# Filter planes of every second frequency group added on the Pool engine and turned in one pass a step later

## Chip, cores and metric

The kernel runs on one core of one Trainium2 chip. The metric is device time in microseconds (us): 248.57 us, the median of three runs (247.84 to 250.53). The core has five engines with queues of their own: TensorE (PE in the profile, with its weight loads as PEld), VectorE (DVE), ScalarE (ACT), GpSimd (POOL) and SyncE (SP), which here issues most DMA transfers. Each engine works through its instructions in the order in which the program wrote them; they wait for each other through semaphores.

## The reference

One transformer block on x of 2048 rows by 640 columns, in bf16:

```python
mod = (_silu(c) @ w_mod)                 # six vectors of 640: sa, ca, ga, sb, cb, gb
h = _layernorm(x, axis=-1) * (1 + ca) + sa
X = rfft2(h, axes=(rows, columns)) * (w_r + 1j * w_i)     # 2048 x 321 filter
x = x + ga * irfft2(X)
h = _layernorm(x, axis=-1) * (1 + cb) + sb
x = x + gb * ((_silu(h @ w_gate) * (h @ w_up)) @ w_down)  # 640 -> 1728 -> 640
```

So there is a spectral filter (a two-dimensional Fourier transform, a product with a complex filter, the transform back) and then a gated feed-forward layer.

## The kernel before

The transforms are matmuls with tables. Up to about 33 us the kernel normalises x and transforms its rows and most of the columns; from about 61 us to 79 us it transforms back and adds into x; after that come the gate, up and down products of the feed-forward layer. What is changed lies between, from 33 to 61 us, and is called the join here: for each column frequency l (0 to 80) the last small transform along the rows is made, the filter applied, and the first small transform back is made.

The frequencies lie in NG = 21 groups of mostly four (group 4 has two, group 5 three). The loop over g (line 764) writes the instructions out step by step; step g works on several groups at once:

- `mix(g+2)` (L581): one matmul of 192 columns per frequency, four per group, into two PSUM banks; the pair of banks is chosen by the group's parity.
- `prod(g+2, .., hl)` (L605, twice): DVE multiplies that result with the filter in `Wt` (tile rW) and writes three planes to SBUF, `PPs` (tile rM). With three real planes a complex product needs three multiplications instead of four; two sums of neighbouring planes are its real and its imaginary part.
- `stage_b(g)` (L613): PE turns the group's products, frequency on frequency, into bank 0 or 1 by a matmul with the identity. It makes two passes that accumulate, so that the planes are summed on the way: 8 matmuls of 128 columns. ACT copies the result to `Y2` (L616).
- `stage_c(u)` (L643) takes a unit of two groups two steps after its second group: 8 matmuls, into banks 6 and 7 for most units, which one copy (`evac`, L652, mostly ACT) then empties into tile rE.

Other work is laid between these:

- `turn` (L381, its copies L387 on ACT) mirrors raw filter rows, through banks 6 and 7. The last two, for l from 64 on, stand in step 6.
- `wsum` (L424, POOL) makes the third plane of the filter, a sum. `sp_gather` (L661, POOL) needs the result of a DMA transpose. L785 and L791 on POOL prepare tables of the next stage.
- `ga_mod` (L713, copy L719) in steps 1 and 2 uses banks 7 and 6.
- `mod_col` (L594): columns of sb and cb (five of each, five matmuls per column), all within `mix` of groups 18 to 20; those of gb in step 20.
- `sp_mm` / `sp_ev`: one special row frequency, in steps 5, 9, 11 and 13 (its parts 3, 0, 1, 2). Part 2 ends with a DMA from SP (L707); behind it in SP's order stand the loads of w_down, w_gate and w_up.
- `sp_w` / `sp_wc`: eight small transposes in step 3 with their copies (L445).

PP has four buffers, Y2 four, and the two banks of `stage_b` alternate. `presum` and `Qs` are in the code already, but `PRE` is empty, so nothing calls them.

Of the kernel before, what the change touches and what calls it, by code (L numbers as in the profile page):

```python
# [11 lines left out]
BF16 = mybir.dt.bfloat16  # L12
# [9 lines left out]
NC5 = 5  # L22
# [144 lines left out]
def adaln_block_kernel(ctx, tc, A_x, A_w_r, A_w_i, B_x, B_w_gate, B_w_up, B_w_down, c, w_mod, out):  # L167
    nc = tc.nc
# [19 lines left out]
    rE = _Region(big, "rE", 40960, "E")  # L188
# [37 lines left out]
    wm_r = rM.cut(12800, [NC5, 4, D])  # L226
# [16 lines left out]
    Wsp = rE.cut(34064, [3, 2, NT, 2], parts=81)  # L243
# [89 lines left out]
    if True:  # L333
# [87 lines left out]
        def wsum(lo, hi, rk, eng):  # L421
            for off in (lo, 161 - hi):
                v = [_rev(Wt, WP * i + 321 * rk + off, [[321, 8], [160, 2], [1, hi - lo]]) for i in range(3)]
                eng.tensor_tensor(v[1], v[2], v[0], ALU.add)  # L424
# [7 lines left out]
                                  sa4[:].unsqueeze(2).unsqueeze(3).to_broadcast([P, 4, 2, 8]))  # L432

        def sp_w():
            tp = psum[0:81, 4, 192:256].bitcast(BF16).rearrange("p (v h a k) -> p v h a k", v=2, h=2, a=2)
            for v in range(2):
                for hl in range(2):
                    for a in range(2):
                        o = 160 * (1 - a if hl else a)
                        nc.tensor.transpose(tp[:, v, hl, a], (Wrev if hl else Wrow)[:, v, o:o + 81], identb[0:16, 0:16])  # L440
            return tp

        def sp_wc(tp):
            for v in range(2):
                nc.vector.tensor_copy(Wsp[:, 2 * v].rearrange("p h k a -> p h a k"), tp[:, v])  # L445
            nc.gpsimd.tensor_tensor(Wsp[:, 1], Wsp[:, 0], Wsp[:, 2], ALU.add)

        cps = psum[:, 3, 0:NC5]
# [32 lines left out]
        dve, act = nc.vector.tensor_copy, nc.scalar.copy  # L481
# [51 lines left out]
    NG = len(groups)  # L533
    if True:
# [40 lines left out]
        def mix(g):  # L575
            ls = groups[g]
            n = len(ls)
            xps = banks(2 + 2 * (g % 2), 2, [4, 256])
            for i, l in enumerate(ls):
                B2, j = B2of[l][0:2]  # L580
                nc.tensor.matmul(xps[:, i, 0:192], lhsT=B2[:, j, :], rhs=KS2, start=True, stop=True)  # L581
                if i == 0:
                    for c5 in {NG - 3: (0, 1), NG - 2: range(NC5), NG - 1: (2, 3, 4)}.get(g, ()):
                        mod_col(psum[:, 2 + 2 * (g % 2), 192 + c5:193 + c5], wm_r[:, :, 1 + g % 2], c5)
            return xps

        def stage_a(g):
            xps = mix(g)
            prod(g, xps, 0)
            prod(g, xps, 1)  # L590

        def mod_col(o, w, c5):
            for k in range(NC5):
                nc.tensor.matmul(o, lhsT=w[:, k, 128 * c5:128 * c5 + 128], rhs=sc_col[:, k:k + 1],  # L594
                                 start=(k == 0), stop=(k == NC5 - 1))
# [11 lines left out]
        def stage_b(g, PP):  # L607
            n = len(groups[g])
            yps = banks((g + 1) % 2, 1, [4, 128])
            Q = Qs.pop(g, None)  # L610
            for ps in (1, 0) if Q is None else (0,):
                for i in range(n):
                    nc.tensor.matmul(yps[:, i, :], lhsT=_rev(PP if Q is None else Q, 64 * n * ps + i, [[n, 128]]), rhs=identb[:],  # L613
                                     start=(i == 0 and (ps == 1 or Q is not None)), stop=(ps == 0 and i == n - 1))
            Y2 = rY.cut(4096 if g == 4 else 1024 * (g % 4), [4, 128])
            nc.scalar.copy(Y2[:, 0:n, :], yps[:, 0:n, :])  # L616
# [28 lines left out]
        def evac(u):  # L645
            g, l0 = units[u][0], groups[units[u][0]][0]
            if g == NG - 2:
                nc.vector.tensor_copy(ep_views(l0, 4), banks(0, 1, [4, 128])[0:127].rearrange("p i q -> p q i"))
            elif g == NG - 1:
                nc.scalar.copy(ep_views(l0, 4), banks(1, 1, [4, 128])[0:127].rearrange("p i q -> p q i"))  # L650
            else:
                (nc.vector.tensor_copy if g == NG - 6 else nc.scalar.copy)(  # L652
                    ep_views(l0 // 4 * 4, 8), banks(4 if g == NG - 4 else 6, 2, [8, 128])[0:127].rearrange("p i q -> p q i"))

        B2sp = rE.cut(20480, [82])
# [7 lines left out]
        def gap(parts, i, w, b):  # L663
            return psum[0:parts, b + i // 2, 192 + 256 * (i % 2):192 + 256 * (i % 2) + w]
# [26 lines left out]
        def sp_ev(i, g):  # L691
            b = 2 + 2 * (g % 2)
            if i == 3:
                for h in range(2):
                    nc.vector.tensor_scalar_mul(SA[:, 41 * h:81 - 40 * (1 - h)], gap(128, h, 41 - h, b), 256.0)
            elif i == 0:
                for v in range(3):
                    nc.vector.tensor_tensor(PPsp[:, 64 * v:64 * v + 64], gap(81, v, 64, b),
                                            Wsp[:, v].rearrange("p h k a -> p (h k a)"), ALU.mult)
            elif i == 1:  # L700
                for h in range(2):
                    ls = slice(41 * h, 41 + 40 * h)
                    nc.scalar.copy(Y2sp[:, ls], gap(128, h, ls.stop - ls.start, b))
            elif i == 2:
                for h in range(2):
                    nc.scalar.copy(Osp[:, 40 * h:40 * h + 40], gap(128, h, 40, b))
# [57 lines left out]
        for g in range(NG + 1):  # L764
            if g == 9:
                nc.gpsimd.tensor_copy(sgnc[:], Kstab[:, 576:577])
# [12 lines left out]
            if 1 < g < NG - 2 and g + 2 in PRE:  # L779
                presum(g + 2)  # L780
            if g in (4, 9):
                wsum(64, 80, 8 * (g // 9), nc.gpsimd)
            if g in (11, 12):
                h4 = slice(4 * (g - 11), 4 * (g - 11) + 4)
                nc.gpsimd.tensor_scalar(sgn_H[:, h4, 1], sgn_H[:, h4, 0], sgnc[:, 0:1], 1.0, ALU.mult, ALU.mult)  # L785
            if g == NG - 3:
                nc.vector.tensor_copy(modcols[:, 2, :], psum[:, 2, 192:197])
                nc.vector.tensor_scalar_add(one_p_cb[:], psum[:, 4, 192:197], 1.0)
            if g in (14, 16):
                i = (16 - g) // 2  # L790
                nc.gpsimd.tensor_tensor(RI[:, i], RI[:, i], ga_bc[:], ALU.mult)  # L791
# [612 lines left out]
```

## Time and profile before

| | |
|---|---|
| median of the runs | 248.57 us (247.84 to 250.53) |
| the profiled execution: its time | 248.34 us |
| the profiled execution: its span | 246.3 us (2.0 us lie around it) |
| granted TensorE clock | 1.0 |
| busy in the whole span | PE 239.1, DVE 203.4, ACT 171.2, POOL 70.9 us |
| from 33 to 60 us | in most stretches of 1 us PE is busy for the whole of it; the weakest is 44 to 45 us with 0.69 |

A row of the timeline gives the start of a group of equal instructions, the time from its first start to its last end, the engine, the line and operation, output and input, how many, and in brackets how long the engine had stood idle before and what released it. PE's matmuls overlap each other: what a group costs PE is read from the start of one group to the start of the next. In lists by line, the three numbers are the shortest, middle and longest duration in ns.

### The profile page before, as it was taken

Reading aid. Unit: us, or ns where it says so; the run is one execution under the profiler, and the core shown is the slowest. Engines: PE = TensorE matmul, PEld = TensorE weight load, DVE = VectorE, ACT = ScalarE, POOL = GpSimd, SP = SyncE. Lnnn points to the kernel's source line nnn. Section 1 sums busy time; section 2 is a strip of 40 time slices with the busy share of each in tenths; the row PEclk is TensorE's granted clock in tenths of the full one; section 3 lists DMA queues with packets and bytes.
Section 4 is the critical chain, followed back from the end, with each engine's and each line's share of the span. In section 5 each row is a group of like instructions: output and inputs, shape, how many; then the busy total and the mean of one; then the engine's idle time right before and its main releaser. Section 6 shows DMA issues by size and latency. Waiting matters only on the chain.

```text
span 246.3 us, 6008 instructions
## 1 busy us (share of the span) xinstructions
PE 239.1 (97%) x2262; PEld 187.8 (76%) x2262; DVE 203.4 (83%) x479; ACT 171.2 (69%) x343; POOL 70.9 (29%) x116
## 2 busy tenths in 40 slices
PE   8889999999999999999999999999999999999994
PEld 2678889999998887788887778887765666656773
DVE  4798777897499996989989968788998777789964
ACT  4789887998988797588864588765247777773220
POOL 4368896660424523002004400001422000004400
PEclk9999999999999999999999999999999999999999
DMA  6999979969999999500005110202411000000111
GB/s 204 381 339 290 342 179 179 253 234 293 289 374 266 194 266 190 123 3 1 3 0 106 59 53 3 53 0 43 86 38 53 0 1 3 0 0 4 53 53 53
DMA packets 44142, 31.19 MB, mean 127 GB/s; under 512 B 21873, under 2 KB 41810, under 8 KB 44114
## 3 DMA queue, kind: packets, MB, share of 16 engines
q1 hardware_dynamic: 42176, 26.15, 39.8%
q0 software_dynamic: 1376, 4.26, 7.5%
q10 hardware_dynamic: 562, 0.41, 0.6%
q8 instruction: 17, 0.28, 0.5%
q14 instruction: 11, 0.09, 0.1%
HBM read 23.49 MB, written 2.62 MB: 106 GB/s over the span
## 4 chain that ended last, share of the span: by engine, by line
PE 84%; DMA 5%; DVE 4%; POOL 2%; ACT 2%; issue 1%; ACTq 0%; DVEq 0%; POOLq 0%
PE psum L1125 36%; PE psum L996 19%; PE psum L1095 6%; PE psum L613 4%; PE psum L973 3%; DMA rW<-rL 3%; PE psum L581 3%; PE psum L404 2%; DMA rX<-in_A_x_dram 2%; PE psum L643 2%; PE psum L1083 2%; DVE bn6a L337 2%; PE psum L729 1%; ACT rE L407 1%; DVE rE L369 1%; POOL rW L879 1%
## 5 line engine op out<-in xcount | busy, mean ns | idle before, releaser
L1125 PEld LDWEIGHTS <-rW 128*128 128x128 bf16 (+1 forms) x429 | 41.9, 98 | 12.6
L1125 PE MATMUL psum<-rW 128*128 128x256 bf16 (+1 forms) x247 | 42.2, 287 | 0.0
L1022 POOL TENSOR_TENSOR rM<-rM,rL 128x320 f32<-128x320 f32 x6 | 5.5, 909 | 97.1 <-ACT rL L1021 97.1
L996 PEld LDWEIGHTS <-rE 128*128 128x128 f16 (+1 forms) x196 | 18.9, 97 | 8.0 <-DVE rE L950 0.3
L605 DVE TENSOR_TENSOR rM<-psum,rW 128x384 bf16<-128x384 f32 (+2 forms) x42 | 20.5, 543 | 4.0 <-PE psum L581 2.7
L996 PE MATMUL psum<-rE 128*128 128x320 f16 (+1 forms) x147 | 22.9, 299 | 0.0
L1163 ACT COPY rX<-psum 128x384 f32<-128x384 f32 (+2 forms) x27 | 14.0, 519 | 7.4 <-PE psum L1125 7.3
L1156 ACT COPY rH<-psum 128x384 f32<-128x384 f32 (+2 forms) x27 | 14.0, 517 | 7.2 <-PE psum L1125 6.5
L1125 PEld LDWEIGHTS <-rE 128*128 128x128 f16 x156 | 15.3, 98 | 4.7
L1160 DVE TENSOR_TENSOR rH<-psum,rM 128x512 bf16<-128x512 f32 (+1 forms) x24 | 15.0, 624 | 4.1 <-PE psum L1125 2.2
L1179 ACT ACTIVATE rL<-psum 128x384 bf16<-128x384 f32 (+2 forms) x27 | 14.4, 533 | 5.4 <-PE psum L1125 3.4
L1164 DVE TENSOR_TENSOR rX<-psum,rX 128x384 f32<-128x384 f32 (+2 forms) x27 | 16.3, 604 | 1.6 <-ACT rX L1163 1.4
L1150 ACT COPY rM<-psum 128x384 f32<-128x384 f32 (+2 forms) x27 | 13.9, 516 | 4.0 <-PE psum L1125 3.9
L1271 DVE SCALAR_TENSOR_TENSOR rM<-psum,rX 128x640 f32<-128x640 f32 x16 | 13.1, 821 | 3.9 <-ACT rL L733 2.4
L1125 PE MATMUL psum<-rW,rE 128*128 128x256 bf16 (+1 forms) x78 | 15.6, 290 | 0.0
L1125 PE MATMUL psum<-rE,rY 128*128 128x256 f16 (+1 forms) x78 | 15.6, 290 | 0.0
L1180 ACT ACTIVATE rL<-rX 128x384 bf16<-128x384 f32 (+2 forms) x27 | 15.1, 558 | 0.0
L337 DVE BATCH_NORM_STATS2 bn6a<-rX 128x6 f32<-128x320 bf16 x30 | 13.1, 480 | 2.4 <-DMA rX<-in_A_x_dram 2.4
L1095 PE MATMUL psum<-rW 128*128 128x256 bf16 x130 | 14.4, 273 | 0.0
L965 DVE TENSOR_TENSOR rA<-psum,rM 128x320 bf16<-128x320 f32 (+1 forms) x27 | 12.1, 472 | 2.4 <-PE psum L973 2.3
L424 POOL TENSOR_TENSOR rW<-rW 128x256 bf16<-128x256 bf16 x20 | 13.5, 704 | 1.4 <-DMA rW<-in_A_w_r_dram 0.7
L1095 PEld LDWEIGHTS <-rW 128*128 128x128 bf16 x130 | 12.7, 98 | 1.5
(231 smaller groups left out, 633.0 us busy)
## 6 DMA issues: line engine op xcount, KB each, us to landing
rM<-in_w_mod_dram SPq DMA_DIRECT2D x4, 800.0 KB, 8.1
out_dram<-rA SPq DMA_DIRECT2D x31, 80.0 KB, 1.6
rX<-in_A_x_dram SPq DMA_DIRECT2D x6, 320.0 KB, 6.3
rA<-in_B_w_down_dram SPq DMA_DIRECT2D x2, 960.0 KB, 6.3
rY<-in_B_w_gate_dram POOLq DMA_DIRECT2D x2, 832.0 KB, 7.8
rW<-in_B_w_gate_dram SPq DMA_DIRECT2D x1, 1440.0 KB, 10.0
rW<-in_A_w_i_dram SPq DMA_DIRECT2D x2, 642.0 KB, 11.1
rW<-in_A_w_r_dram SPq DMA_DIRECT2D x2, 642.0 KB, 10.5
```

The lines of the kernel that those rows point to most:

```text
L337: nc.vector.bn_stats(bn6a[:, i % 2, k, :], x_sb[:, i, 320 * k:320 * k + 320])
L605: nc.vector.tensor_tensor(PPs[g][:, v0:v1, hl], xv[:, v0:v1, hl], in1, ALU.mult)
L996: nc.tensor.matmul(o, lhsT=lhs[rows(k), k], rhs=rhs[rows(k), k], start=start and k == ks[0], stop=stop and k == ks[-1], skip_group_check=True)
L1095: nc.tensor.matmul(gu[u], lhsT=Wgu[:, u, c5, ff * 128:(ff + 1) * 128], rhs=h2T[:, :, c5, :], start=(c5 == 0), stop=(c5 == NC5 - 1))
L1125: nc.tensor.matmul(o[:, f], lhsT=w, rhs=b, start=(start and f == 0 and i == 0), stop=(stop and f == len(groups[g]) - 1 and i == len(ops) - ...
L1150: nc.scalar.copy(c0, X)
L1156: nc.scalar.copy(c2, X)
L1160: nc.vector.tensor_tensor(c11, Z, c0, ALU.add)
L1163: nc.scalar.copy(c3, X)
L1164: nc.vector.tensor_tensor(c22, Y, c3, ALU.add)
L1179: nc.scalar.activation(g21, X, ACT.Silu, scale=-1.0)
L1180: nc.scalar.activation(g22, c22, ACT.Silu, scale=-1.0)
```

## The change

Three things are done to the join.

1. For the odd groups 3 to 17 (`PRE`), `presum` adds the two sums of planes on POOL into `Q` (tile rE, three buffers in turn), one instruction of 128x512 each, behind the group's products. `stage_b` of these groups then takes one pass, 4 matmuls instead of 8.
2. For groups 3 to 17, odd and even (`LAGS`), `stage_b` stands one step later: in step g it is written for group g-1. Step 3 has none and step 18 has two. `stage_c` stays where it was, so it comes one step behind the `stage_b` of its second group instead of two.
3. Other work moves. The last two `turn` go from step 6 to steps 7 and 9; `wsum` of rows 32 to 47 from ahead of the loop to step 2, that of 64 to 79 from steps 4 and 9 to 10 and 12; L785 from steps 11 and 12 to 14 and 18; L791 from 14 and 16 to 16 and 17; the ten `mod_col` of sb and cb from `mix` of groups 18 to 20 to those of groups 8, 10, 12, 14, 16 (one each), 18 (two) and 20 (three), now all in bank 3; `ga_mod` stands ahead of `stage_b`; `sp_w` goes from step 3 to step 5 with its transposes in bank 1, and its copies from DVE to ACT; the copies of the special row's parts 1 and 2 go from ACT to DVE, ahead of the step's products.

```diff
-            tp = psum[0:81, 4, 192:256].bitcast(BF16)...
+            tp = psum[0:81, 1, 256:320].bitcast(BF16)...
...
-                nc.vector.tensor_copy(Wsp[:, 2 * v]..., tp[:, v])
+                nc.scalar.copy(Wsp[:, 2 * v]..., tp[:, v])
...
-                    for c5 in {NG - 3: (0, 1), NG - 2: range(NC5), NG - 1: (2, 3, 4)}.get(g, ()):
-                        mod_col(psum[:, 2 + 2 * (g % 2), 192 + c5:193 + c5], wm_r[:, :, 1 + g % 2], c5)
+                    for c5 in {8: (0,), 10: (1,), 12: (2,), 14: (3,), 16: (4,), 18: (5, 6), 20: (7, 8, 9)}.get(g, ()):
+                        mod_col(psum[:, 3 + 2 * (g % 2), 448 + c5:449 + c5], wm_r[:, :, 1 + c5 // NC5], c5 % NC5)
...
-            Qs[g] = rE.cut(21504 + 1024 * (g % 3), [m])
+            Qs[g] = rE.cut(21504 + 1024 * (PRE.index(g) % 3), [m])
...
-                    nc.scalar.copy(Y2sp[:, ls], ...)
+                    nc.vector.tensor_copy(Y2sp[:, ls], ...)
...
-                    nc.scalar.copy(Osp[:, 40 * h:40 * h + 40], ...)
+                    nc.vector.tensor_copy(Osp[:, 40 * h:40 * h + 40], ...)
...
-        PRE = set()
-        SPG = (9, 11, 13, 5)
+        PRE = (3, 5, 7, 9, 11, 13, 15, 17)
+        LAGS = range(3, 18)
+        SPG = (9,11,13,5)
...
-        wsum(32, 48, 8, nc.gpsimd)
...
-                if g == 3:
-                    tp = sp_w()
-                stage_a(g + 2)
-                if g == 3:
-                    sp_wc(tp)
-                if g in SPG:
+                xps = mix(g + 2)
+                if g in SPG and SPG.index(g) in (1, 2):
                     sp_ev(SPG.index(g), g)
-            if 1 < g < NG - 2 and g + 2 in PRE:
+                prod(g + 2, xps, 0)
+                prod(g + 2, xps, 1)
+                if g == 2:
+                    wsum(32, 48, 8, nc.gpsimd)
+                if g in SPG and SPG.index(g) not in (1, 2):
+                    sp_ev(SPG.index(g), g)
+            if g + 2 in PRE:
                 presum(g + 2)
-            if g in (4, 9):
-                wsum(64, 80, 8 * (g // 9), nc.gpsimd)
-            if g in (11, 12):
+            if g in (10, 12):
+                wsum(64, 80, 8 * (10, 12).index(g), nc.gpsimd)
+            if g in (14, 18):
...
-            if g in (14, 16):
-                i = (16 - g) // 2
+            if g in (16, 17):
+                i = 1 - (16, 17).index(g)
                 nc.gpsimd.tensor_tensor(RI[:, i], RI[:, i], ga_bc[:], ALU.mult)
-            if g < NG:
-                Y2s[g] = stage_b(g, PPs.pop(g))
+            if 0 < g < 3:
+                ga_mod(320 * (2 - g), 8 - g)
+            for b in (g - 1, g):
+                if 0 <= b < NG and (b in LAGS) == (b < g):
+                    tp = sp_w() if b == 4 else None
+                    Y2s[b] = stage_b(b, PPs.pop(b))
+                    if b == 4:
+                        sp_wc(tp)
+            if g in (7, 9):
+                i = (7, 9).index(g)
+                turn(64, i, 6 + i, act)
             if g == 0:
                 stage_a(3)
-            if 0 < g < 3:
-                ga_mod(320 * (2 - g), 8 - g)
-            if g == 6:
-                turn(64, 0, 6, act)
-                turn(64, 1, 7, act)
```

More of the change, by code (lines that the diff above doesn't have):

```diff
@@ L434, in sp_w @@
         def sp_w():
-            tp = psum[0:81, 4, 192:256].bitcast(BF16).rearrange("p (v h a k) -> p v h a k", v=2, h=2, a=2)
+            tp = psum[0:81, 1, 256:320].bitcast(BF16).rearrange("p (v h a k) -> p v h a k", v=2, h=2, a=2)
             for v in range(2):
@@ L444, in sp_wc @@
             for v in range(2):
-                nc.vector.tensor_copy(Wsp[:, 2 * v].rearrange("p h k a -> p h a k"), tp[:, v])
+                nc.scalar.copy(Wsp[:, 2 * v].rearrange("p h k a -> p h a k"), tp[:, v])
             nc.gpsimd.tensor_tensor(Wsp[:, 1], Wsp[:, 0], Wsp[:, 2], ALU.add)
@@ L651, in evac @@
             else:
-                (nc.vector.tensor_copy if g == NG - 6 else nc.scalar.copy)(
+                (nc.vector.tensor_copy if g in (15,) else nc.scalar.copy)(
                     ep_views(l0 // 4 * 4, 8), banks(4 if g == NG - 4 else 6, 2, [8, 128])[0:127].rearrange("p i q -> p q i"))
@@ L702, in sp_ev @@
                     ls = slice(41 * h, 41 + 40 * h)
-                    nc.scalar.copy(Y2sp[:, ls], gap(128, h, ls.stop - ls.start, b))
+                    nc.vector.tensor_copy(Y2sp[:, ls], gap(128, h, ls.stop - ls.start, b))
             elif i == 2:
                 for h in range(2):
-                    nc.scalar.copy(Osp[:, 40 * h:40 * h + 40], gap(128, h, 40, b))
+                    nc.vector.tensor_copy(Osp[:, 40 * h:40 * h + 40], gap(128, h, 40, b))
                 nc.sync.dma_start(Em[127:128].rearrange("p v q c -> p (v q c)").rearrange("p (a n) -> p a n", n=64), Osp[:, 0:64].unsqueeze(1))
@@ L780, in adaln_block_kernel @@
+                if g == 2:
[3 more added lines that the diff above has]
+            if g + 2 in PRE:
                 presum(g + 2)
-            if g in (4, 9):
-                wsum(64, 80, 8 * (g // 9), nc.gpsimd)
-            if g in (11, 12):
-                h4 = slice(4 * (g - 11), 4 * (g - 11) + 4)
+            if g in (10, 12):
+                wsum(64, 80, 8 * (10, 12).index(g), nc.gpsimd)
@@ L785, in adaln_block_kernel @@
+            if g in (14, 18):
+                h4 = slice(4 * (14, 18).index(g), 4 * (14, 18).index(g) + 4)
                 nc.gpsimd.tensor_scalar(sgn_H[:, h4, 1], sgn_H[:, h4, 0], sgnc[:, 0:1], 1.0, ALU.mult, ALU.mult)
             if g == NG - 3:
-                nc.vector.tensor_copy(modcols[:, 2, :], psum[:, 2, 192:197])
-                nc.vector.tensor_scalar_add(one_p_cb[:], psum[:, 4, 192:197], 1.0)
-            if g in (14, 16):
-                i = (16 - g) // 2
+                nc.vector.tensor_copy(modcols[:, 2, :], psum[:, 3, 448:453])
+                nc.vector.tensor_scalar_add(one_p_cb[:], psum[:, 3, 453:458], 1.0)
```

## The prediction

> **What bounds the kernel now.** I read the page's busy times first, then the chain that ended last, and then the timeline of each engine from 31 to 63 us, where the change lies.
>
> ```profile
> PE 239.1 (97%) x2262; PEld 187.8 (76%) x2262; DVE 203.4 (83%) x479; ACT 171.2 (69%) x343; POOL 70.9 (29%) x116
> ```
>
> PE is the bound of the whole, and the chain agrees: from 35.4 to 69 us it lies on PE but for one short detour. PE's timeline shows that detour, around the two turns of step 6:
>
> ```profile
> 43.05 0.49 PE L581 MATMUL psum<-Ktab,rL 128*128 128x192 bf16 x4
> 43.38 0.61 PE L613 MATMUL psum<-identb,rM 128*128 128x128 bf16 x8
> 44.31 0.64 PE L381 MATMUL psum<-rW,flipb 128*128 128x256 bf16 x4 [0.32 <-ACT rE L652]
> 44.79 0.49 PE L581 MATMUL psum<-Ktab,rL 128*128 128x192 bf16 x4
> 45.12 0.61 PE L613 MATMUL psum<-identb,rM 128*128 128x128 bf16 x8
> 45.56 0.49 PE L581 MATMUL psum<-Ktab,rL 128*128 128x192 bf16 x4
> ```
>
> From start to start, four mix matmuls cost 0.33 us (44.79 to 45.12) and the eight of stage_b 0.445 (45.12 to 45.56), 55.6 ns each; stage_c's eight cost the same 0.445. At 44.31 PE had been free since 43.83 and waited for ACT to empty banks 6 and 7.
>
> But PE is not alone. A pair of steps costs PE 2 x 0.33 + 2 x 0.445 + 0.445 = 2.0 us. The timelines of ACT and DVE give their sides:
>
> ```profile
> 53.18 1.09 ACT L616 CAST rY<-psum 128x512 bf16<-128x512 f32 x2
> 54.14 1.05 ACT L652 CAST rE<-psum 127x1024 bf16<-127x1024 f32 x1
> 55.04 1.14 ACT L616 CAST rY<-psum 128x512 bf16<-128x512 f32 x2
> ```
>
> ```profile
> 48.82 2.86 DVE L605 TENSOR_TENSOR rM<-psum,rW 128x384 bf16<-128x384 f32 x6
> ```
>
> ACT's pair is 55.04 - 53.18 = 1.86 us (two Y2 copies 0.96, one evac 0.90). DVE's six products start 0.463 apart ((2.86 - 0.547)/5), four in a pair make 1.85. PE is thus ahead of the next engine by 0.15 us a pair only; beyond that a saving on PE is not a saving of time.
>
> **The change, part by part.**
>
> *Fewer turns.* One pass instead of two saves 4 matmuls in each of seven groups and 3 in group 5: 31, with their weight loads. 31 x 55.6 ns = 1.72 us off PE. **-1.72.**
>
> *mod_col.* 50 matmuls of 23.4 ns (25 take 0.60 us) are moved, not saved: 1.18 us leave the mixes of groups 18 to 20, 0.117 us comes to five earlier mixes and 0.58 us stays late. The sum over PE is 0; it fills the room that the turns leave. The first cb column now stands in step 16. Its weights are issued at 45.4 and land 7.3 us later, at 52.7; that step's mix starts at 54.32 now, so PE would have to be 1.5 us ahead there to wait for them.
>
> *The wait at 44.31 goes* (-0.48), and so do three small ones around 51.1, 51.6 and 53.0 (0.10, 0.07 and 0.18), where Y2 copies stood on ACT behind the copies of the special row: those go to DVE, 0.2 to 0.3 us each, inside DVE's waits for PE (0.2 to 0.7 us per pair of steps). I take -0.3. **-0.78 together.**
>
> *New waits.* They replace the one removed:
> - ga_mod now stands ahead of stage_b in step 1. Its bank 7 is free when the copies L387 end at 37.11 (35.88 + 1.23); PE gets there at 36.80, because the eight turns that covered it now come behind. **+0.35.**
> - The turn in step 7 needs bank 6. The evac ahead of it ended at 44.26, and ACT, dense there, is not earlier. PE comes at 45.56 (today's end of step 7) - 0.48 (wait) - 0.48 (turns) - 0.445 (group 7 lags) - 0.39 (seven matmuls fewer) + 0.12 (mod_col) + 0.35 (ga_mod) = 44.23. **+0.1.**
> - Counted from that turn's start T, PE comes to stage_c of step 8 at T+0.91 (turn 0.24, mix 0.33, mod_col 0.12, one-pass stage_b 0.22). Its bank 6 holds the turn until ACT has made the Y2 copy ahead of it (to T+0.68) and two L387 copies (0.70): T+1.42 with the semaphore. **+0.5.** Before, a whole step lay between.
> - That stage_c (nine matmuls, 0.5, and 0.16 from the last start to completion: 219 ns less 56) is complete at T+2.08, its evac (1.02) at T+3.12. PE reaches the second turn, which needs bank 7, in step 9 at T+1.92 + 0.11 (special row) + 0.33 + 0.445 = T+2.81. **+0.35.**
> - From step 10 a ring runs through ACT: second half of stage_c (0.22 + 0.16 to completion), evac 0.92, Y2 copy of the lagging even group 0.59, two semaphores 0.09: 1.98 us. PE's pair is now 0.66 + 0.22 + 0.445 + 0.445 + 0.12 = 1.89, and 2.0 where the special row is added. With the Pool chain (below) I put this at **+0.25** over steps 10 to 18.
>
> Sum of new waits +1.55. All three engines then stand at 1.85 to 1.98 us a pair: most of the saving meets the next engine.
>
> *Pool.* No row shows an addition of 128x512. The nearest:
>
> ```profile
> L791 POOL TENSOR_TENSOR rH<-rH,ga_bc x2: 1406/1406/1407, 50.5 to 51.8; 128x640 bf16<-128x640 bf16 x2
> ...
> L661 POOL TENSOR_TENSOR rE<-rL,SA x3: 223/227/234, 43.7 to 44.1; 128x16 bf16<-128x16 bf16 x2, 128x15 bf16<-128x15 bf16 x1
> ```
>
> (1406 - 227)/624 = 1.89 ns an element; at 512, 227 + 496 x 1.89 = 1.16 us. The high end is twice the longest wsum of 256 elements (862 ns), 1.72; the low end half of L785's one-input 1.115, 0.56. I take 1.16: same operation, both contiguous. Where does it lie on a path? Pool's timeline:
>
> ```profile
> 45.25 0.98 POOL L661 TENSOR_TENSOR rE<-rM,SA 128x16 bf16<-128x16 bf16 x6 [0.93 <-DMA rM<-rA]
> 46.18 0.19 POOL L766 CAST sgnc<-rE 128x1 f32<-128x1 bf16 x1
> 46.32 1.35 POOL L424 TENSOR_TENSOR rW<-rW 128x256 bf16<-128x256 bf16 x2
> ```
>
> Pool is held until 45.25 by a DMA that the change doesn't move. Behind it now stand presum 9, L766, presum 11, wsum, presum 13, wsum, presum 15, L785, presum 17: from 46.2, with five additions P, 0.14 + 2 x 1.36 + 1.1 + 5P. With 1.16 presum 17 ends at about 56.0, and step 18 needs it; that step's stage_b stands at 57.90 now. So Pool permits a gain of up to 1.9 us there and only touches in steps 16 and 18. The moved tables L785 and L791 end by 60 us; the next stage reads them from 61 us on, and the half moved last only at 70.
>
> A gain or loss from Pool and DVE working at once is bounded by the row of six products above: they ran at 0.463 us while Pool multiplied L785 and L791 (48.3 to 53.2), as at other times. In a later stage, the one w_down fold L909 (both inputs in SBUF) that runs beside Pool's L879 takes 0.73 us instead of 0.48. The Trainium skill, page "SBUF — State Buffer", section "Who interferes with whom", says that DVE and GpSimd exclude each other for a whole instruction when the DVE operation has two SBUF inputs or a two-port mode. By that rule the products, with one input in PSUM, stay free, and the trace agrees (0.463 us beside Pool); the rule would leave the last rival below no chance.
>
> *After the join.* PE runs on without a gap to 79.0, so a shift should be carried along. The next thing that could eat it:
>
> ```profile
> 70.39 7.03 DMA rW<-rL
> ...
> 77.53 2.17 POOL rW L879 x4
> ...
> 79.74 0.38 PE psum L1083 x2
> ```
>
> The transpose of the first normalised rows is issued behind DVE's work, which moves with the join, and competes with weight loads. These start behind the special row's output, today at 53.36; its copies stand ahead of the products of step 13 now, which makes them some 1.3 us earlier. I take this as carried at full, +0.
>
> **Sum.** -1.72 - 0.78 + 1.55 = -0.95 us. On the profiled execution's own 248.34 us (span 246.3 and 2.0 around it) that gives 247.4; the median lies 0.23 above it, so 247.6.
>
> **Rivals.**
> 1. *The whole relief arrives*: ACT reaches the L387 copies and evacs as much earlier as PE, and the new waits stay away. -1.72 - 0.78 = -2.5: 246.1, range 245.9 to 247. For it: ACT idles 2.8 us in all for stage_b's results. Against: ACT's pair of 1.86 is not touched. 0.17.
> 2. *Lost at the feed-forward layer*: the transposed rows land when the queue of loads lets them, at 77.4 as now; PE waits longer at 79. 0, so 248.6. For: that transfer takes 7.03 us, on the chain. Against: the loads ahead of it move too. 0.14.
> 3. *Pool is late* (slower). presum 17 ends at 50.2 + 5P; behind it PE has 1.11 us (stage_b 17 and 18, stage_c) to the mark that stands at 58.79 now. So it decides from P = 1.49 us: each 0.1 above costs 0.5 us. At the high end 1.72 the mark is at 59.9: +1.15, 249.7, and 2 us give +2.5. 0.11.
> 4. *Products and Pool additions block each other*: a pair of steps takes DVE 1.85 + 1.16 = 3.0 instead of PE's 2.2, over six pairs +5: 253. 0.03.
>
> That the change doesn't do what it says I leave out: the order of the changed program has 31 fewer turns and weight loads and eight more Pool additions.
>
> **Chances.** The forecast (-0.2 to -1.6) has 0.55, the rivals as given. One per cent, 2.5 us, is about what a measurement of this kernel can tell from no change. Faster by more: the better half of rival 1, 0.1. Slower by more: rival 4 and the tail of rival 3, with an execution like the 250.53 in the median, 0.08. Within: 0.82. The range 246.0 to 249.9 takes in the forecast, nearly all of rivals 1 and 2 and rival 3 to the high end of P.
>
> **What would show it.** L613 x131 instead of x162; L622 eight times at about 1.16 us (group 5 less); PE waiting for ACT L387 before the first turn of ga_mod and in steps 8 and 9, for 1.2 us or so; no idle PE ahead of two turns in one step; the last matmul of the join some 0.95 us earlier than 61.2. I am wrong if presum comes above 1.4 us, if ACT's waits stay away, or if PE's wait at 79 us grows by what the join gains.

## The result and the profile after

The changed kernel takes 247.84 us (median of 22 runs, 246.43 to 249.27), the kernel before, run beside it, 249.24 us (22 runs, 247.61 to 251.27; the 248.57 us shown ahead is the median of the first three of these). The ratio is 0.9951 with a 95% interval of 0.9927 to 0.9974: 0.6 to 1.8 us less, 1.2 us at the middle. The interval lies below 1, so the kernel is faster, by less than the one per cent that the prediction set as the bound of a clear change. The profiled execution took 247.88 us with a span of 246.1 us, against 248.34 and 246.3.

The two spans differ by 0.2 us only. To see where the gain is, the span has to be cut at marks that both kernels have: the first mix of the join (L581), the first matmul of the transform back (L729), and the first down-table product of the feed-forward layer (L973, L979 after the change; lines behind the loop are six higher now). These are the rows for the three stretches from the join on, first before, then after. The columns are the length, busy time and instructions of PE, its weight loads, DVE, ACT and POOL, the granted clock, the DMA share and GB/s.

```profile
33.61:61.22 27.61, 27.22 (x472) 25.78 (x470) 23.32 (x56) 23.57 (x47) 14.68 (x30) 1.00 0.92 228
61.22:94.69 33.47, 33.20 (x396) 29.92 (x394) 29.19 (x79) 28.85 (x65) 13.17 (x19) 1.00 1.11 272
94.69:246.30 151.61, 148.11 (x1127) 109.19 (x1124) 125.55 (x273) 93.05 (x190) 20.50 (x21) 1.00 0.16 37
```

```profile
34.45:61.16 26.71, 26.16 (x441) 24.02 (x438) 23.23 (x56) 23.61 (x45) 23.36 (x38) 1.00 0.98 244
61.16:94.75 33.59, 33.30 (x396) 29.97 (x394) 29.24 (x79) 28.90 (x65) 13.29 (x20) 1.00 1.12 264
94.75:246.10 151.35, 147.86 (x1127) 109.39 (x1124) 125.24 (x273) 92.94 (x190) 20.73 (x21) 1.00 0.17 37
```

The join is shorter by 0.90 us, the next stretch longer by 0.12, the last shorter by 0.26. Ahead of the join the changed kernel's execution lost 0.84 us (34.45 against 33.61), which nearly hides all that. That loss is not the change's: DVE idled there 3.4 us ahead of the row statistics (L337) for the load of x, against 2.4 us before, and a second execution of the same changed kernel (below) idled 2.2 us and came to the join at 33.29.

From the start of the join to the end of the span it is 212.69 us before and 211.65 after; in a second trace of each (below), 212.71 and 211.41. So the traces show 1.0 and 1.3 us less behind that mark, around the 1.2 of the whole runs.

The share of PE went down by the turns, that of POOL up by the additions:

```profile
PE 236.5 (96%) x2231; PEld 185.8 (75%) x2231; DVE 203.1 (83%) x481; ACT 171.1 (70%) x341; POOL 80.0 (32%) x124
```

By line, of the kernel before and then of the changed one, with the shortest, middle and longest duration in ns:

```profile
L613 PE MATMUL psum<-identb,rM x162: 216/219/220, 36.0 to 59.6; 128*128 128x128 bf16 x162
...
L605 DVE TENSOR_TENSOR rM<-psum,rW x42: 447/547/559, 34.3 to 58.6; 128x384 bf16<-128x384 f32 x38, 128x192 bf16<-128x192 f32 x2, 128x288 bf16<-128x288 f32 x2
```

```profile
L613 PE MATMUL psum<-identb,rM x100: 217/219/231, 36.9 to 59.6; 128*128 128x128 bf16 x100
L613 PE MATMUL psum<-identb,rE x31: 218/219/248, 41.4 to 57.7; 128*128 128x128 bf16 x31
...
L622 POOL TENSOR_TENSOR rE<-rM x8: 912/1154/1163, 39.0 to 56.3; 128x512 bf16<-128x512 bf16 x7, 128x384 bf16<-128x384 bf16 x1
...
L605 DVE TENSOR_TENSOR rM<-psum,rW x42: 448/547/558, 35.0 to 58.2; 128x384 bf16<-128x384 f32 x38, 128x192 bf16<-128x192 f32 x2, 128x288 bf16<-128x288 f32 x2
```

Of 162 turns 131 are left, 31 of them on planes that Pool added. An addition takes 1.154 us (1.16 was estimated), and the products beside it take what they took (547 ns, before and after).

PE's timeline after shows the new waits. Each is read from the start of a group plus its matmuls at 82.5 ns (L581), 55.6 ns (L613) or 0.12 us (L381) to the start of the next.

```profile
37.31 0.49 PE L581 MATMUL psum<-Ktab,rM 128*128 128x192 bf16 x4
37.99 0.84 PE L713 MATMUL psum<-rM,sc_rep 128*128 128x320 bf16 x5 [0.18 <-ACT rW L387]
...
45.93 0.39 PE L613 MATMUL psum<-identb,rE 128*128 128x128 bf16 x4
46.60 0.27 PE L640 MATMUL psum<-Ktab,rY 128*128 128x128 bf16 x2 [0.29 <-ACT rW L387]
...
47.68 0.61 PE L613 MATMUL psum<-identb,rM 128*128 128x128 bf16 x8
48.37 0.40 PE L381 MATMUL psum<-rW,flipb 128*128 128x256 bf16 x2
```

They are 0.35 us ahead of the first gate product (37.64 to 37.99), 0.45 ahead of the pass of step 8 (46.15 to 46.60) and 0.24 ahead of the second turn in step 9 (48.13 to 48.37). The bracket shows less than the gap, because the idle time counts from the modelled end of the last matmul.

Behind these waits the engines run level. These are 6.32 us of the same place in the join, from 14.83 us behind its start, before and then after, with the columns of the stretches above:

```profile
48.44:54.76 6.32, 6.30 (x110) 6.07 (x108) 5.71 (x16) 5.53 (x13) 4.81 (x4) 1.00 0.76 260
```

```profile
49.28:55.60 6.32, 6.32 (x117) 6.09 (x115) 6.32 (x18) 6.15 (x10) 6.28 (x8) 1.00 0.85 259
```

DVE, which still had 0.6 us to spare there, has none left, Pool 0.04 and ACT 0.17 (the same in the second trace of the changed kernel, to within 0.03).

### The profile page after: what moved, and what is told of

Its sections match the earlier page's. It is cut to its first block, busy times and chain, and to the rows that moved or that the text cites. A ratio compares the mean times of both kernels' runs of the same rounds, so it can differ in the third digit from the quotient of the medians.

```text
span 246.1 us, 5962 instructions
## 1 busy us (share of the span) xinstructions
PE 236.5 (96%) x2231; PEld 185.8 (75%) x2231; DVE 203.1 (83%) x481; ACT 171.1 (70%) x341; POOL 80.0 (32%) x124
## 4 chain that ended last, share of the span: by engine, by line
PE 81%; DMA 5%; DVE 4%; POOL 4%; ACT 3%; issue 1%; ACTq 0%; DVEq 0%; POOLq 0%
PE psum L1131 36%; PE psum L1002 19%; PE psum L1101 6%; PE psum L979 3%; DMA rW<-rL 3%; PE psum L581 3%; PE psum L613 2%; PE psum L404 2%; DMA rX<-in_A_x_dram 2%; PE psum L643 2%; PE psum L1089 2%; DVE bn6a L337 2%; ACT rE L407 1%; POOL rL L1284 1%; DVE rE L369 1%
## 5 line engine op out<-in xcount | busy, mean ns | idle before, releaser
L337 DVE BATCH_NORM_STATS2 bn6a<-rX 128x6 f32<-128x320 bf16 x30 | 13.0, 479 | 3.4 <-DMA rX<-in_A_x_dram 3.4
L404 PE MATMUL psum<-rE 128*128 128x256 bf16 x80 | 10.5, 274 | 3.6 <-DVE rE L369 2.5
```

What stands on the lines that cost most here:

```text
L337: nc.vector.bn_stats(bn6a[:, i % 2, k, :], x_sb[:, i, 320 * k:320 * k + 320])
L404: nc.tensor.matmul(zA[:, c5], lhsT=lhsT, rhs=Mtab[:, t, h], start=(h == 0), stop=(h == 1))
```

## The experiments

All lengths of the join come from one profile each. It repeats well: 27.61 and 27.60 for the kernel before, 26.71 and 26.75 for the changed one, while whole runs of one kernel scatter by 3 us. So the join decides between mechanisms, and the ratio of whole runs, with its interval, only bounds the rest.

| kernel | join, us | ratio to before (95%) |
|---|---|---|
| before; again | 27.61; 27.60 | again: 1.0011 (0.9968 to 1.0055) |
| changed; again | 26.71; 26.75 | 0.9951 (0.9927 to 0.9974); 0.9939 (0.9901 to 0.9978) |
| no additions, turns in two passes | 27.79 | 0.9984 (0.9937 to 1.003) |
| each addition made twice | 33.49 | 1.021 (1.0144 to 1.0276) |
| gate products behind the turns | 26.71 | 0.9926 (0.9883 to 0.9969) |
| columns back in groups 18 to 20 | 27.20 | 0.9982 (0.994 to 1.0023) |
| turns in their own step | 28.52 | 0.9987 (0.9962 to 1.0011) |
| sign pass behind the last addition | 26.71 | 0.9948 (0.9929 to 0.9968) |
| both weight turns in step 6 | 26.91 | 0.9942 (0.9912 to 0.9973) |
| gate products in step 4 | 27.28 | 0.9955 (0.9919 to 0.999) |
| before, with the copies' engines changed alone | 27.56 | 0.9976 (0.9939 to 1.0014) |

### The changed kernel again

No edit.

> The changed kernel once more, to see how well the length of the join repeats (from the first matmul of mix to the first matmul L729 of the next stage: 27.61 us before, 26.71 in the one profile of the changed kernel). If the length is set by the order of the instructions and their durations, as both theories below say, it comes out within 0.1 us of 26.71, wherever the join begins. If it wanders by several tenths, differences of the join cannot be read from single profiles.

The join lasted 26.75 us, 0.04 more than in the first profile. The gain in the join is no accident of one execution.

### Without the additions

```diff
-        PRE = (3, 5, 7, 9, 11, 13, 15, 17)
+        PRE = ()
```

> The changed kernel without the eight Pool additions: the filter planes are again summed on PE in two passes of stage_b, a step later, and everything else stays where the change put it. PE gets 31 matmuls of 55.6 ns back, 1.72 us. Theory A (PE, ACT and DVE stand nearly level; a saving on PE is partly turned into waits for ACT): the waits shrink again where PE arrives later (0.22 of the 0.45 before stage_c of step 8, most of some 0.3 over steps 10 to 18), so the join grows by about 1.2 us, to 27.9. Rival B (PE alone sets the pace): it grows by the whole 1.72, to 28.4. Rival C (the lag and the moved work bring the gain, the additions nothing): it stays at 26.7 to 27.0.

27.79 us, 1.08 more than with the additions, as the first theory had it (1.2). PE's timeline of this kernel shows that the waits on ACT come with the order of the steps and not with the additions:

```profile
45.63 0.61 PE L613 MATMUL psum<-identb,rM 128*128 128x128 bf16 x8
46.39 0.27 PE L640 MATMUL psum<-Ktab,rY 128*128 128x128 bf16 x2 [0.15 <-ACT rW L387]
...
47.33 0.61 PE L613 MATMUL psum<-identb,rM 128*128 128x128 bf16 x8
48.15 0.40 PE L381 MATMUL psum<-rW,flipb 128*128 128x256 bf16 x2 [0.21 <-ACT rE L652]
```

They are 0.32 us (46.07 to 46.39) and 0.38 (47.77 to 48.15), with the 0.35 of the gate product 1.05 us. In the kernel before the waits that went were 0.86 us: 0.49 ahead of the turns of step 6, and 0.11, 0.07 and 0.19 around 51.1, 51.6 and 53.0 us (51.09 to 51.20, 51.63 to 51.70, 52.91 to 53.10). The difference, +0.19, is the measured +0.18 of the lag and the moves without the additions. The 31 turns saved then bring 1.08 of their 1.72 us. The theory's places are not quite met: without the additions the wait in step 8 is smaller by 0.13 us (it had 0.22), and the one in step 9 larger by 0.14. Most of the 0.64 us lies in gaps of at most 0.11 us, from step 5 on, that only the kernel with the additions has.

### Each addition twice

```diff
-            nc.gpsimd.tensor_tensor(Qs[g], _rev(PPs[g], 0, [[1, m]]), _rev(PPs[g], m // 2, [[1, m]]), ALU.add)
+            for _ in range(2):
+                nc.gpsimd.tensor_tensor(Qs[g], _rev(PPs[g], 0, [[1, m]]), _rev(PPs[g], m // 2, [[1, m]]), ALU.add)
```

> The changed kernel with every Pool addition made twice (the second writes the same sums again), so 2.31 us instead of 1.16 for each. Theory A (Pool is held until a DMA transpose lands, at 46.2 in the profile, and from there runs as a chain of five additions, two sums of the filter and two small operations that ends in step 18 with no slack): five more additions of 1.16 less the 0.6 us that Pool still idled, so the join grows by about 5.2 us, to 31.9, and the time by the same. Rival (Pool lies off the path, half idle as its busy share of 32% suggests): under 1 us.

The join lasted 33.49 us (34.89 to 68.38), 1.6 more than expected, and whole runs 254.12 us (four runs), 7.05 more than the changed kernel on the same chip. The larger ones of PE's waits on Pool in this kernel, whose lines behind 622 are one higher:

```profile
49.19 0.30 PE L677 MATMUL psum<-rE 128*81 128x64 bf16 x3 [0.82 <-POOL rE L662]
...
57.67 0.41 PE L613 MATMUL psum<-identb,rE 128*128 128x128 bf16 x4 [1.46 <-POOL rE L623]
61.33 0.41 PE L613 MATMUL psum<-identb,rE 128*128 128x128 bf16 x4 [1.44 <-POOL rE L623]
```

Pool as the bound is real, and sets in earlier than I had counted: the additions of groups 5 and 7 are late as well (PE idles 0.28 and 0.53 us for them) and push the special row's gather (L662) back, ahead of the mark from which I had summed. With one addition none of this is there.

### Gate products behind the turns

The two calls of `ga_mod` stand behind `stage_b` again, as in the kernel before.

```diff
-            if 0 < g < 3:
-                ga_mod(320 * (2 - g), 8 - g)
...
+            if 0 < g < 3:
+                ga_mod(320 * (2 - g), 8 - g)
```

> The changed kernel with ga_mod of steps 1 and 2 behind stage_b again, as it stood before the change. Theory A (PE waits 0.35 us for the copies L387 in step 1 because ga_mod comes too early, and nothing in these steps needs it early): the wait goes and the join shrinks by 0.35 us, to 26.35. Rival (the join is held further on by ACT or Pool, and an earlier PE waits there instead): 26.6 to 26.8.

26.71 us: the rival. The wait of 0.35 us ahead of the first gate product is gone, and one of 0.43 us stands in step 3 (the three mixes from 40.40 on hold PE to 40.65), since the pass there takes the banks that the gate copies have yet to empty:

```profile
40.40 0.41 PE L581 MATMUL psum<-Ktab,rL 128*128 128x192 bf16 x3
41.08 0.44 PE L643 MATMUL psum<-Ktab,rY 128*128 128x128 bf16 x5 [0.27 <-ACT ga_bc L719]
```

### Columns back in groups 18 to 20

```diff
-                    for c5 in {8: (0,), 10: (1,), 12: (2,), 14: (3,), 16: (4,), 18: (5, 6), 20: (7, 8, 9)}.get(g, ()):
-                        mod_col(psum[:, 3 + 2 * (g % 2), 448 + c5:449 + c5], wm_r[:, :, 1 + c5 // NC5], c5 % NC5)
+                    for c5 in {NG - 3: (0, 1), NG - 2: range(NC5), NG - 1: (2, 3, 4)}.get(g, ()):
+                        mod_col(psum[:, 2 + 2 * (g % 2), 192 + c5:193 + c5], wm_r[:, :, 1 + g % 2], c5)
```

> The changed kernel with its modulation columns back in the mixes of groups 18 to 20; everything else as changed, no work left out. The columns are the same PE work in either place. Theory: the spread columns are what PE does while Pool makes its additions. Seven of the ten stood ahead of the turn of group 17 in the changed kernel, at about 0.13 us each, so that PE comes to that turn 0.9 us earlier while the addition of group 17 still ends where it did (57.46 us in the changed kernel's own trace, with PE there 0.06 us behind it): a wait of about 0.7 us on Pool appears at the turns of groups 13 to 17 together, and the join lasts 27.2 to 27.5 us instead of 26.71. Rival: where the columns stand is indifferent, since PE is the bound in all steps alike: 26.6 to 26.8 us.

27.20 us: the length is the theory's, at the edge of its range, but the place is not. The one wait on Pool is 0.17 us, at the turn of group 15. The pass of step 8 now waits 0.59 us for ACT (44.77 to 45.36) where it waited 0.45, and 0.14 to 0.25 us are lost in or behind the passes of steps 8 to 14, where there were 0.10 at most. For the largest of these (0.25, step 10) the trace names ACT, for that of step 8 (0.20) DVE, and for the two of 0.14 nothing.

```profile
44.55 0.39 PE L613 MATMUL psum<-identb,rE 128*128 128x128 bf16 x4
45.36 0.27 PE L640 MATMUL psum<-Ktab,rY 128*128 128x128 bf16 x2 [0.41 <-ACT rW L387]
```

So columns of 0.12 us laid into the early steps are hidden there behind waits that exist anyway, and 0.5 us of them cost nothing. What holds PE in those steps is mostly ACT, and not Pool.

### Turns in their own step

```diff
-        LAGS = range(3, 18)
+        LAGS = ()
```

> The changed kernel with every turn in its own step instead of one step later; the additions on Pool stay and are turned in one pass. No work left out. Theory: Pool is nearly full in the join (23.36 of 26.71 us), so its additions end at the same times, and PE, which comes to each turn one step (about 1.2 us) earlier, waits for Pool: some 0.8 us at group 9, less at 11, about 1.1 us at 15 and 17, each taking the earlier ones in; the join lasts 27.6 to 28.1 us, so that nearly all the gain of the single pass is lost. Rival: the additions are early enough anyway and the lag only keeps buffers longer: 26.5 to 26.8 us.

28.52 us, 1.81 more than the changed kernel and 0.9 more than the kernel before. PE waits on Pool, the first time here:

```profile
43.86 0.49 PE L581 MATMUL psum<-Ktab,rL 128*128 128x192 bf16 x4
44.95 0.41 PE L613 MATMUL psum<-identb,rE 128*128 128x128 bf16 x4 [0.60 <-POOL rE L622]
```

0.76 us at group 7 (44.19 to 44.95), 0.67 at group 13, 0.49 at 15 and 0.17 at 17. The theory holds, with a larger loss than expected and partly at other groups: I had put it at 9 and 11, and the most at 15 and 17. The lag is what makes the additions worth anything. The whole runs (0.9987) are lower than a join 0.9 us longer would give even with the 0.25 us that the last two experiments explain; what makes up the rest isn't settled.

### Sign pass behind the last addition

```diff
-            if g in (14, 18):
-                h4 = slice(4 * (14, 18).index(g), 4 * (14, 18).index(g) + 4)
+            if g in (16, 18):
+                h4 = slice(4 * (16, 18).index(g), 4 * (16, 18).index(g) + 4)
```

> The changed kernel with Pool's sign pass of step 14 (1.10 us) laid behind the addition of group 17 (step 16). No work left out. Theory: Pool is the last to arrive at the turn of group 17 alone, by no more than 0.1 us; the addition of 17 now ends 1.1 us earlier and the join shortens by 0.05 to 0.15 us, to 26.55 to 26.7 us. Rival: from step 12 on Pool's chain holds PE at every odd group's turn, and the join shortens by 0.3 us or more, to 26.4 us or less.

26.71 us, no change; I had expected at least 0.05 less. Pool's timeline of the changed kernel, and then of this one:

```profile
55.23 1.10 POOL L787 TENSOR_SCALAR rH<-rH,sgnc 128x1024 bf16<-128x1024 bf16 x1
56.31 1.15 POOL L622 TENSOR_TENSOR rE<-rM 128x512 bf16<-128x512 bf16 x1
```

```profile
54.85 1.16 POOL L622 TENSOR_TENSOR rE<-rM 128x512 bf16<-128x512 bf16 x1 [0.37 <-DVE rM L605]
55.98 1.12 POOL L787 TENSOR_SCALAR rH<-rH,sgnc 128x1024 bf16<-128x1024 bf16 x1
```

In the changed kernel the last addition ends at 57.46 and PE's turn starts at 57.52; here Pool has time to wait for DVE, ends at 56.01, and PE still turns group 17 at 56.72. In both PE has no gap ahead of that turn above 0.04 us. Pool arrives just in time, and its arrival costs nothing.

### Both weight turns in step 6

```diff
-            if g in (7, 9):
-                i = (7, 9).index(g)
-                turn(64, i, 6 + i, act)
+            if g == 6:
+                turn(64, 0, 6, act)
+                turn(64, 1, 7, act)
```

> The changed kernel with both weight turns back in step 6, as in the kernel before, instead of steps 7 and 9. No work left out. Theory: the waits of 0.45 us at the pass of step 8 and of 0.24 us at the turn of step 9 come from ACT's copies of the turns, which share banks 6 and 7 with those passes; with both turns in step 6, two steps ahead of the pass, both waits go and about 0.3 us comes in step 6 for the copy of step 5's pass: the join lasts 26.2 to 26.5 us. Rival: PE, earlier by that, only waits further on for ACT or Pool, as it did when the gate products were laid behind the turns: 26.65 to 26.8 us.

26.91 us, worse than both had it. The waits of steps 8 and 9 do go, but the one in step 6 is as large as they were (three turns from 45.02, so 45.19 to 45.87: 0.68 us):

```profile
45.02 0.33 PE L613 MATMUL psum<-identb,rE 128*128 128x128 bf16 x3
45.87 0.64 PE L381 MATMUL psum<-rW,flipb 128*128 128x256 bf16 x4 [0.53 <-ACT rE L652]
```

It lies ahead of the mixes of groups 9 to 11, and so moves the addition of group 11 from 14.70 to 14.94 us behind the join's start. The additions of 13 to 17 follow without slack, and PE waits 0.18 us for that of group 15. A wait late in a step costs itself; one ahead of the mixes costs Pool as well.

### Gate products in step 4

Both `ga_mod` calls are taken out of steps 1 and 2 and stand behind `stage_b` of step 4.

```diff
-            if 0 < g < 3:
-                ga_mod(320 * (2 - g), 8 - g)
...
+            if g == 4:
+                ga_mod(320, 7)
+                ga_mod(0, 6)
```

> The changed kernel with both gate products (ten matmuls of 320 columns, 1.36 us on PE) taken out of steps 1 and 2 and laid behind the turn of group 4 in step 4, where banks 6 and 7 lie between the passes of steps 3 and 5. No work left out. Theory: the wait of 0.35 us for ACT's copies of the first turns goes, and a wait of at most 0.1 us on the copy of step 3's pass comes in its place: the join lasts 26.3 to 26.5 us. Rival: in steps 1 and 2, without that work, PE runs ahead of DVE's products (0.93 us a step against 0.78 us of PE) and of Pool's first addition, and the pass of step 5 waits for ACT, which then has the two gate copies (0.42 us each) just ahead of it: the join lasts 26.65 us or more.

27.28 us: the rival's length, by more than it asked, though the pass of step 5 doesn't wait, as the rival had it. DVE's products are dense from 35.62 to 40.54 us, and PE, with nothing between, has gaps of 0.22, 0.18 and 0.11 us there; then 0.48 us (39.60 to 40.08) for the copy of step 3's pass, and in step 9 0.39 us instead of 0.24:

```profile
35.62 4.92 DVE L605 TENSOR_TENSOR rM<-psum,rW 128x384 bf16<-128x384 f32 x11
```

```profile
39.38 0.42 PE L613 MATMUL psum<-identb,rE 128*128 128x128 bf16 x4
40.08 1.52 PE L713 MATMUL psum<-rM,sc_rep 128*128 128x320 bf16 x10 [0.28 <-ACT rE L652]
```

### The kernel before again

No edit; it was run for the 0.26 us behind the join.

> The kernel before, unchanged, for a second trace of it. In its first trace the join lasted 27.61 us, the part from the first down-table product of the feed-forward layer (L973) to the end of the span 151.61 us, and the transpose of the normalised rows 7.03 us with a wait of PE behind it. All other kernels so far had 151.35 to 151.39 us in that part. If the 0.25 us there belong to the kernel before, this run has 151.6 us again, and some of what the changed kernel gains as a whole lies outside the join; if they belong to that one execution, it has 151.3 to 151.4 us. The join should repeat to within 0.05 us (27.56 to 27.66), and the transpose come anywhere between 5.3 and 7.0 us, as it did in two executions of the changed kernel (6.96 and 5.8).

The join lasted 27.60 us and the last stretch 151.59, against 151.35 to 151.39 in every traced kernel that holds the change or most of it. So 0.25 us outside the join belong to the kernel before. The trace of DVE shows where: ahead of L1182 it pauses in two places, though what it works on is there. Its timeline before and then after (L956 and L1182 there are L962 and L1188 here):

```profile
169.60 0.29 DVE L956 TENSOR_TENSOR rE<-rX,rE 128x256 f16<-128x256 bf16 x1
169.94 0.43 DVE L1182 TENSOR_TENSOR rX<-rH,rL 128x512 bf16<-128x512 bf16 x1
...
222.87 0.28 DVE L956 TENSOR_TENSOR rE<-rM,rE 128x256 f16<-128x256 bf16 x1
223.41 0.36 DVE L1182 TENSOR_TENSOR rM<-rH,rL 128x384 bf16<-128x384 bf16 x1 [0.26 <-DVE rE L956]
```

```profile
169.66 0.28 DVE L962 TENSOR_TENSOR rE<-rX,rE 128x256 f16<-128x256 bf16 x1
169.87 0.42 DVE L1188 TENSOR_TENSOR rX<-rH,rL 128x512 bf16<-128x512 bf16 x1
...
222.80 0.28 DVE L962 TENSOR_TENSOR rE<-rM,rE 128x256 f16<-128x256 bf16 x1
223.07 0.36 DVE L1188 TENSOR_TENSOR rM<-rH,rL 128x384 bf16<-128x384 bf16 x1
```

From start to start it takes 0.34 us instead of 0.21, and 0.54 instead of 0.27. The down products that wait for that result come 0.11 to 0.12 us later at each place.

### The copies' engines alone

In the kernel before, the special row's copies go to DVE and the copies L445 to ACT, as in the change; nothing else. DVE has two instructions more by it, 481, as many as in the changed kernel.

```diff
-                nc.vector.tensor_copy(Wsp[:, 2 * v].rearrange("p h k a -> p h a k"), tp[:, v])
+                nc.scalar.copy(Wsp[:, 2 * v].rearrange("p h k a -> p h a k"), tp[:, v])
...
-                    nc.scalar.copy(Y2sp[:, ls], gap(128, h, ls.stop - ls.start, b))
+                    nc.vector.tensor_copy(Y2sp[:, ls], gap(128, h, ls.stop - ls.start, b))
...
-                    nc.scalar.copy(Osp[:, 40 * h:40 * h + 40], gap(128, h, 40, b))
+                    nc.vector.tensor_copy(Osp[:, 40 * h:40 * h + 40], gap(128, h, 40, b))
```

> The kernel before with one part of the change alone: the copies of the special row (L703, L706) on DVE instead of ACT, and the copies L445 of step 3 on ACT instead of DVE. No work left out, and like the changed kernel it gives DVE two instructions more than the kernel before. Join, theory: the three small waits of PE around 51.1, 51.6 and 53.0 us (0.11, 0.07 and 0.19 us) go and nothing takes their place, so that the join lasts 27.2 to 27.35 us instead of 27.60; rival: DVE's products of steps 11 and 13 come 0.2 to 0.3 us later behind the copies and PE waits for them, 27.5 us or more. Part from the first down-table product to the end of the span: 151.35 us if the two short pauses of DVE there (0.13 and 0.27 us ahead of L1182) hang on where its instructions lie in its stream, which two more ahead of them would move as in the changed kernel; 151.6 us if they hang on something else that the change touched.

The profiled execution's span is 250.0 us, longer ahead of the join and at the transposed rows, so only the two stretches of the expectation are read.

```profile
35.89:63.45 27.56, 27.18 (x472) 25.71 (x469) 23.12 (x56) 23.51 (x45) 14.71 (x30) 1.00 0.93 224
98.62:250.00 151.38, 147.87 (x1127) 109.38 (x1124) 125.09 (x272) 93.06 (x190) 20.45 (x21) 0.99 0.16 37
```

```profile
226.68 0.28 DVE L956 TENSOR_TENSOR rE<-rM,rE 128x256 f16<-128x256 bf16 x1
226.94 0.36 DVE L1182 TENSOR_TENSOR rM<-rH,rL 128x384 bf16<-128x384 bf16 x1
```

The pauses are gone (0.26 us from start to start here, 0.20 at the first place) and the last stretch is 151.38 us: with two more instructions on DVE, which ran 100 us and more ahead of them, they don't come. The same edit takes two instructions from ACT (341 for 343), so the count on DVE is not all that differs. In the join the length is the rival's (27.5 or more), its mechanism isn't. The three small waits go, as the theory said, but the L445 copies delay ACT in step 3 and PE waits 0.22 us for the next pass; the join is only 0.04 us shorter. In the changed kernel these copies stand in step 5.

## Why the prediction was right

**Where the time went.** 1.2 us less as a whole, 0.95 forecast. The join gave 0.90, as forecast. Another 0.25 us is DVE's two pauses, which no step of the prediction has: a gain by accident, which the move of the copies brings by itself (the last experiment), without the additions. That the forecast of 247.6 us came so near to the 247.84 is partly luck: the median of before was 0.7 us higher over 22 runs than over the first three, and this second gain made up for some of that.

**Term by term**, in us:

| term | predicted | in the trace |
|---|---|---|
| 31 turns fewer | -1.72 | matmuls in the join 472 to 441, at 55.6 ns: -1.72 |
| waits gone | -0.78 | 0.49 + 0.11 + 0.07 + 0.19: -0.86 |
| first gate product | +0.35 | +0.35 |
| turn in step 7 | +0.1 | none ahead of it, 0.09 behind it |
| pass of step 8 | +0.5 | +0.45, and 0.10 behind it |
| turn in step 9 | +0.35 | +0.24 |
| steps 10 to 18 | +0.25 | 0.07 + 0.09 + 0.10: +0.26 |
| sum | -0.95 | -1.09; the join -0.90 |

The 0.19 us between the listed terms and the join lie in gaps under 0.1 us, which I didn't follow one by one. Two terms were off: the turn of step 9 by 0.11, since PE came to it 2.98 us behind the first turn instead of 2.81, and the waits gone by 0.08.

**"Beyond 0.15 us a pair a saving on PE is not a saving of time"** carries the result. By it eight pairs would have room for about 1.2 us of a saving (8 x 0.15); the 31 turns brought 1.08 of their 1.72, and DVE, ACT and Pool are then as full as PE (the rows of 6.32 us above). Three kernels took a wait from PE or moved it (gate products in two places, weight turns), and the join came out at 26.71, 27.28 and 26.91: in none did the room become time. Each of them also brought a wait of its own, of 0.43 to 0.68 us, so they show that these waits can't be moved away, but not by themselves that level engines are the reason. The whole relief (the first rival, -2.5 us) falls with that.

**Pool.** The addition was estimated at 1.16 us and takes 1.154; the last ends at 57.46 with PE there at 57.52, so "only touches" was right, and moving Pool's sign pass showed that the touch costs nothing. The chain's end was not: the prediction's 56.0 us lie 22.4 behind the start of the join, and Pool was done 23.0 behind it, since it stood idle for DVE for 0.74 us ahead of the addition at 49.15, which the sum leaves out. It permitted 1.3 us there and not 1.9. The third rival's point of decision, 1.49 us, wasn't met; making the addition twice showed its mechanism, and its price for a far larger addition was set too low: by 0.5 us for each 0.1 above 1.49, 2.31 us give 4.1, and the join grew by 6.8; Pool was then late ahead of the gather as well.

**Products and additions at once** (the fourth rival): 547 ns a product before and after. The rule that the prediction named, from the Trainium skill's page "SBUF — State Buffer", section "Who interferes with whom", agrees with it for eight additions beside products with one input in PSUM.

**After the join.** From its end to PE's wait for the transposed rows it is 18.52 us before and 18.64 after, so the gain is carried on but for 0.1, and the second rival falls for this pair of traces. But the transfer itself is not fixed: it took 6.96 us in the changed kernel's first execution, with a wait of PE behind it, and 5.8 us in the second, with none. There the stretch behind the join lasted 33.31 us, 0.16 less than the 33.47 of both traces of the kernel before. Whether the change is behind that, two traces of each kernel can't tell.

**Rearrangements.** None of the versions tried beats the changed kernel: the best joins equal its 26.71 us.

## What to carry to other kernels

When the engines beside the bound have only a few per cent of room, list for each saving the next engine's ring and price it; here 1.72 us of turns and 0.86 us of old waits met about 1.5 us of new ones. Where work is handed to another engine, the step of lag between its result and its use is what makes it worth doing: without it the same additions cost 0.9 us instead of bringing 0.9. And cut two traces at common marks before comparing them: the spans, 0.2 us apart, hid a loss of 0.84 that was chance, and two gains that repeat, one of them not planned.

## What the runs showed of the hardware that was not expected

DVE's pauses of 0.13 and 0.27 us in the middle of a dense stretch go with how many instructions lie ahead in its stream: with 479 in all they were there in both traces, with 481 in none of the eleven others, among them the kernel before with other copies alone. The Trainium skill, page "Runtime: NRT & Kernel Launch", section "Instruction fetch mechanics", says that each engine's instructions are fetched in blocks while it runs, and that crossing into a new block is mostly hidden. The traces have such fetches, as DMA packets of the kind "instruction" (queue q14, 8 KB each). In both traces with the pauses one starts 1.0 us behind the start of L956 at the first place, and 1.5 and 1.2 us behind it at the second; in all eleven others one starts 1.2 to 1.5 us ahead of that line at the first place and 0.5 to 0.8 us at the second. So a fetch moves together with the pauses, and the runs fit a crossing that is not quite hidden. But the packet starts when the pause is over, and the trace doesn't say for which engine it is, so that this is the cause isn't shown.

The same DMA transpose of the normalised rows took 5.3 to 8.2 us in thirteen executions, 7.0 in both of the kernel before. Where it took 7.0 (three executions) PE waited 0.25 us at the gate's last products, and where it took 8.2 it waited four times, 1.4 us together; at 6.5 us it waited 0.12 us, and up to 6.2 us not at all.
